# PSUM buffers for the turned x in an RWKV-6 and MLP-mixer kernel: from the pair shared with token mixing to the state products' or the grams'

## Chip, cores, metric

One core of one Trainium2 chip. The metric is the device time of one execution in microseconds, the median of several.

## The reference

```python
B, H, S, D = 4, 8, 768, 48                       # r, k, v, w: (B, H, S, D); DM = H * D = 384
for t in range(S):                               # RWKV-6, per batch and head
    cur = u * k[t] (outer) v[t]
    y[t] = r[t] @ (state + cur)
    state = w[t][:, None] * state + k[t] (outer) v[t]
x = y transposed to (B, S, H * D)
h = relu(x.T @ w_tok1) @ w_tok2                  # token mixing, d_tok = 256
u = x + h.T
out = u + relu(u @ w_ch1) @ w_ch2                # channel mixing, d_ch = 1536
```

All in fp32.

## The kernel before

It first runs the attention of batch 0 (three units of 256 tokens; twelve units in all), then for each batch the mixer, with the next batch's attention woven among it. Three pools of PSUM take all eight banks of 2 KiB (abridged; comments are mine):

```python
ps_g = tile_pool(name="ps_g", bufs=2, PSUM)   # grams: 2 buffers of [128, 2, 512] fp32, two banks each
ps_a = tile_pool(name="ps_a", bufs=1, PSUM)   # state products kv and y: 1 buffer of two banks
ps_m = tile_pool(name="ps_m", bufs=2, PSUM)   # all the rest, tag "m": 2 buffers of one bank
```

The stage of the change, for each batch `bt` (abridged; comments are mine, L428 is line 428 of the kernel):

```python
def back(c):                                  # token mixing's second product, row c (128 tokens), C = 6 rows
    ps = ps_m.tile([128, DM], f32, name="h_ps", tag="m")
    for i in range(DTOK // 128):
        pe.matmul(ps, wtok2[:, i, ts(c, 128)], h1[:, i, :], start=(i == 0), stop=(i == DTOK // 128 - 1))  # L428
    x = xs[bt]
    dve.tensor_add(x[:, c, :], x[:, c, :], ps)                                                            # L430

def turn(c):                                  # turn row c of x, for the channel products
    ps = ps_m.tile([128, DM // 128, 128], f32, name="xT_ps", tag="m")
    for m in range(DM // 128):
        pe.transpose(ps[:, m, :], xs[bt][:, c, ts(m, 128)], ident)                                        # L435
    act.copy(xT[:, :, ts(c, 128)], ps)                                                                    # L436

def up(s, jt):                                # channel mixing's first product
    ps = ps_m.tile([128, SEG], f32, name="z_ps", tag="m")                                                 # L443, L445
    ...
turned = [(1.3, lambda: back(0))]
for c in range(1, C):
    turned += [(1.3, lambda c=c: back(c)), (0.6, lambda c=c: turn(c - 1))]
turned.append((0.6, lambda: turn(C - 1)))
```

So the order is product 0, product 1, transposes 0, product 2, transposes 1, ... product 5, transposes 4, transposes 5. Then come channel products (`z_ps`) and "quarter products" (`q_ps`, `quarters`, channel mixing's second product with seven products instead of eight). The attention parts that are woven among these are small matmuls (48*64, 48*32 and 64*64 in the profile's rows, where the mixer's are 128*128): `gram`, products of k with r (L233, L250, L256), `kv_ps`, k with v for the state (L333), and `y_ps`, the attention's result (L370, L383). The turned k (`kT_ps`, L323) is a 128*128 transpose. Each engine's order is fixed when the kernel is compiled, and pieces of later work are then put where a gap is expected, as the traces show.

## Time and profile before

| | before |
|---|---|
| time, median of six runs in all | 626.71 us (625.52 to 629.18) |
| span of the profiled run | 624.1 us |
| PE idle after the first 90 us | 4.1 + 5.0 us |
| PE, batches 1 and 2, in the stage | 14.16 of 14.24, 15.86 of 16.15 us busy |

A row of the timeline gives start, length, engine, line, operation, operands, count and, in brackets, the idle time of the engine before it with what ended it. PE matmuls are pipelined: the length of a row runs to the modelled end of the last one. In the trace, one fp32 matmul of the source is two records. The page and views are in the prediction below.

### The profile page before, as it was taken

How to read it: one execution, taken by the hardware profiler on the slowest of the kernel's cores; microseconds unless marked ns; L12 is line 12 of the kernel's file. 1: busy time of each engine (PE TensorE's matmuls, PEld its weight loads, DVE VectorE, ACT ScalarE, POOL GpSimd, SP SyncE). 2: the span in 40 equal slices, each digit the busy share in tenths (PEclk: the TensorE clock that was granted, in tenths of full speed). 3: DMA queues.
4: the chain of work that ended last, by engine and by line, in shares of the span. 5: the costliest groups of instructions: out<-in, count | busy, mean ns of one | idle time of the engine just before them, and what ended most of it. 6: DMA issues, size and time to landing. Idle time of an engine off the chain costs nothing.

```text
span 624.1 us, 19852 instructions
## 1 busy us (share of the span) xinstructions
PE 591.5 (95%) x8980; PEld 500.7 (80%) x8980; DVE 341.5 (55%) x743; ACT 201.6 (32%) x500; POOL 7.2 (1%) x32
## 2 busy tenths in 40 slices
PE   2888788999999999999999999999999999999997
PEld 2867556876888896789889896789899885898987
DVE  5889799996766783436364362526243331040403
ACT  6064554520355433432323312332212411202020
POOL 4000000000000000000000000000000000000000
PEclk9996679999999999999999999999999999999999
DMA  8236564610232222111111100000000000000000
GB/s 344 105 80 213 162 197 141 221 43 27 65 94 79 54 67 66 30 50 27 53 45 60 27 28 27 1 2 3 26 2 27 2 27 1 0 1 26 16 12 26
DMA packets 19380, 38.63 MB, mean 62 GB/s; under 512 B 2112, under 2 KB 12864, under 8 KB 19296
## 3 DMA queue, kind: packets, MB, share of 16 engines
q1 hardware_dynamic: 19152, 37.36, 19.0%
q8 instruction: 70, 1.15, 0.8%
q14 instruction: 14, 0.11, 0.1%
q10 hardware_dynamic: 144, 0.00, 0.0%
HBM read 32.64 MB, written 4.72 MB: 60 GB/s over the span
## 4 chain that ended last, share of the span: by engine, by line
PE 88%; DVE 6%; ACT 3%; issue 1%; DMA 1%; SPq 0%; DVEq 0%; ACTq 0%
PE z_ps L443 30%; PE q_ps L477 25%; PE gram L256 8%; PE h_ps L428 5%; PE h_ps L421 5%; PE h_ps L453 3%; PE y_ps L383 2%; PE y_ps L370 2%; PE kv_ps L333 2%; PE gram L233 2%; PE kT_ps L323 1%; PE xT_ps L435 1%; PE gram L250 1%; DVE state L350 1%; DMA w<-in_rkw_dram 1%
## 5 line engine op out<-in xcount | busy, mean ns | idle before, releaser
L443 PE MATMUL z_ps<-xT,wch 128*128 128x256 f32 x864 | 195.3, 382 | 0.0
L443 PEld LDWEIGHTS z_ps<-xT,wch 128*128 128x128 f32 x864 | 161.4, 190 | 22.4 <-ACT z L445 0.7
L445 ACT ACTIVATE z<-z_ps 128x256 f32<-128x256 f32 x144 | 55.0, 382 | 159.4 <-PE z_ps L443 145.7
L477 PE MATMUL q_ps<-wch,z 128*128 128x192 f32 x528 | 93.6, 329 | 0.0
L477 PEld LDWEIGHTS q_ps<-wch,z 128*128 128x128 f32 x528 | 86.3, 190 | 1.3
L477 PE MATMUL q_ps<-scratch,z 128*128 128x192 f32 x396 | 71.1, 330 | 0.0
L256 PEld LDWEIGHTS gram<-r,k 48*64 48x64 f32 x3072 | 59.4, 153 | 13.0 <-issue 7.2
L256 PE MATMUL gram<-r,k 48*64 48x32 f32 x3072 | 64.6, 235 | 4.1 <-issue 1.8
L477 PEld LDWEIGHTS q_ps<-scratch,z 128*128 128x128 f32 x396 | 64.3, 190 | 0.9 <-ACT kT L324 0.2
L288 DVE TENSOR_TENSOR k<-k,decay 112x512 f32<-112x512 f32 x36 | 24.9, 691 | 46.1 <-PE gram L256 34.6
L469 DVE TENSOR_TENSOR z<-z 128x768 f32<-128x768 f32 x11 | 10.5, 958 | 63.5 <-ACT z L445 63.4
L288 DVE TENSOR_TENSOR k<-k,w 112x512 f32<-112x512 f32 x36 | 24.8, 690 | 35.6 <-PE gram L256 30.0
L428 PE MATMUL h_ps<-h,wtok 128*128 128x384 f32 x96 | 37.0, 510 | 3.8 <-DVE x L430 2.0
L350 DVE SCALAR_TENSOR_TENSOR state<-state,w_chunk,kv_ps 128x48 f32<-128x48 f32 x160 | 30.7, 258 | 17.3 <-PE kv_ps L333 17.3
L421 PE MATMUL h_ps<-x,wtok 128*128 128x384 f32 x96 | 37.5, 541 | 1.7 <-ACT x L389 1.6
L430 DVE TENSOR_TENSOR x<-x,h_ps 128x384 f32<-128x384 f32 x24 | 13.3, 555 | 36.6 <-PE h_ps L428 36.3
L233 PE MATMUL gram<-rp,kp 48*64 48x64 f32 x768 | 22.5, 248 | 10.9 <-ACT kp L221 8.2
L272 DVE COPY_PREDICATED at<-mask,gram 128x512 f32<-128x512 uint8 x36 | 32.3, 898 | 0.0
L233 PEld LDWEIGHTS gram<-rp,kp 48*64 48x64 f32 x768 | 18.4, 154 | 15.4 <-ACT kp L221 10.7
L421 PEld LDWEIGHTS h_ps<-x,wtok 128*128 128x128 f32 x96 | 19.2, 208 | 13.5 <-ACT x L389 2.0
L280 ACT COPY at<-gram 16x256 f32<-16x256 f32 x48 | 17.4, 363 | 36.3 <-PE gram L256 35.1
L428 PEld LDWEIGHTS h_ps<-h,wtok 128*128 128x128 f32 x96 | 16.4, 189 | 15.5 <-DVE x L430 3.3
(80 smaller groups left out, 563.0 us busy)
## 6 DMA issues: line engine op xcount, KB each, us to landing
scratch<-in_w_ch_dram SPq DMA_DIRECT2D x10, 512.0 KB, 4.4
vt<-in_v_dram SPq DMA_DIRECT2D x12, 384.0 KB, 3.7
out_dram<-o SPq DMA_DIRECT2D x24, 192.0 KB, 1.9
x<-in_w_ch_dram SPq DMA_DIRECT2D x8, 512.0 KB, 4.4
w<-in_rkw_dram SPq DMA_DIRECT2D x18, 192.0 KB, 3.3
k<-in_rkw_dram SPq DMA_DIRECT2D x18, 192.0 KB, 3.1
r<-in_rkw_dram SPq DMA_DIRECT2D x18, 192.0 KB, 3.5
scratch<-in_w_tok_dram SPq DMA_DIRECT2D x4, 512.0 KB, 9.2
```

Source lines behind the costliest of these rows:

```text
L233: pe.matmul(g[cols, q, ts(a, T)], L["kp"][rows, tokens], L["rp"][rows, tokens], start=True, stop=True)
L256: fours(lambda q, j, rows, cols: pe.matmul(g[cols, q, ts(ca, 32)], k_[rows, ds(ca * 128 + j * T, T)], right[rows, ts(2 * ca + j, 32 // b), ...
L272: dve.copy_predicated(out=dst, data=g.rearrange("p q (m b) -> p q m b", b=b), mask=masks[l].rearrange("p x t -> p (x t)").rearrange("p (m ...
L280: act.copy(at[p:p + b, :, :, n * 2 * b + b:(n + 1) * 2 * b], g[p:p + b, :, :, ts(n, b)])
L288: dve.tensor_mul(left, left, wv[:, :, 1].unsqueeze(2).to_broadcast([ROWS, n, b]))
L350: dve.scalar_tensor_tensor(new[:, a], state[bt, g][:, a], L["w"][:, c, a, j:j + 1], got[:, a], op0=ALU.mult, op1=ALU.add)
L421: pe.matmul(sums[i], wtok1[:, c, ts(i, 128)], xs[bt][:, c, :], start=(c == 0), stop=(c == C - 1))
L428: pe.matmul(ps, wtok2[:, i, ts(c, 128)], h1[:, i, :], start=(i == 0), stop=(i == DTOK // 128 - 1))
L443: pe.matmul(ps, wch1[:, m, ts(jt, 128)], xT[:, m, ts(s, SEG)], start=(m == 0), stop=(m == DM // 128 - 1))
L445: act.activation(zs[s][:, jt, :], ps, AF.Relu)
L453: pe.matmul(ps, zs[0][:, jt, ts(n, 128)], wch2[:, jt, :], start=(jt == 0), stop=(jt == NJ - 1))
L477: pe.matmul(ps, a[:, j, :], b[:, j, :], start=(j == 0), stop=(j == HJ - 1))
```

## The change

Intent: the product gets both small buffers for itself, so that its addition no longer holds up the next product; the transposes borrow a buffer that is free at the time. In batches 0 and 3 no attention runs beside this stage and the state buffer is free; in batches 1 and 2 state products of the next batch run there, so a gram buffer is taken.

```diff
         def turn(c):
-            ps = ps_m.tile([128, DM // 128, 128], f32, name="xT_ps", tag="m")
+
+            if bt in (0, B - 1):
+                ps = ps_a.tile([128, 2, 512], f32, name="xT_ps", tag="a")
+            else:
+                ps = ps_g.tile([128, 2, 512], f32, name="xT_ps", tag="gram")
+            ps = ps[:, 0, :DM].rearrange("p (m t) -> p m t", t=128)
             for m in range(DM // 128):
```

## The prediction

> **What bounds the kernel now.** I read first the page's busy shares and its picture by slices, and the two agree: TensorE is the bound nearly everywhere after the first 90 us.
>
> ```profile
> PE 591.5 (95%) x8980; PEld 500.7 (80%) x8980; DVE 341.5 (55%) x743; ACT 201.6 (32%) x500; POOL 7.2 (1%) x32
> ...
> PE   2888788999999999999999999999999999999997
> ...
> DVE  5889799996766783436364362526243331040403
> ...
> PEclk9996679999999999999999999999999999999999
> ```
>
> PE is idle 624.1 - 591.5 = 32.6 us in all. Cutting the span into three stretches shows where:
>
> ```profile
> 0.00:90.00 90.00, 66.61 (x1874) 54.92 (x1874) 75.26 (x175) 43.58 (x105) 6.66 (x27) 0.85 0.57 185
> 90.00:520.00 430.00, 425.86 (x6598) 357.61 (x6597) 241.70 (x524) 139.93 (x351) 0.56 (x5) 1.00 0.16 48
> 520.00:624.10 104.10, 99.06 (x511) 88.15 (x509) 24.54 (x45) 18.11 (x46) 0.00 (x0) 1.00 0.03 12
> ```
>
> The columns are the stretch, its length, then busy time of PE, PEld, DVE, ACT, POOL, the granted clock, the DMA share and GB/s. 23.4 us of the idle time lie in the first 90 us, before the changed code is first reached (its first transpose runs at 92.2 us); the change cannot touch them. Only 4.1 us lie between 90 and 520, and 5.0 us after 520 (some of that is the end of the program). So the purse is small from the start. The table of waits, restricted to PE, says which waits the changed code owns:
>
> ```profile
> PE h_ps L428 <- DVE x L430: 2.0, 6, 0.4
> ...
> PE h_ps L428 <- ACT xT L436: 1.7, 3, 0.6
> ...
> PE xT_ps L435 <- ACT xT L436: 0.6, 1, 0.6
> ...
> PE xT_ps L435 <- DVE x L430: 0.3, 1, 0.3
> ```
>
> L428 is token mixing's second product (24 of them, six for each of four batches), L430 the VectorE addition that empties it, L435 the transposes of a row of x, L436 the ScalarE copy that empties them. Products and transposes now take turns in two PSUM buffers of one bank each, which the hidden product, the channel products and, in batches 1 to 3, the turned k share too. These rows hold 4.6 us of plain idleness, but the modelled end of a pipelined matmul hides part of a wait, so I measured the steps themselves in the timeline. In the last batch, where nothing else runs beside it:
>
> ```profile
> 523.72 1.56 PE L428 MATMUL h_ps<-h,wtok 128*128 128x384 f32 x4 [0.32 <-DVE x L430]
> 524.79 0.14 PEld L435 LDWEIGHTS xT_ps<-ident,x 128*128 128x128 f32 x1
> 525.11 0.49 PE L435 MATMUL xT_ps<-ident,x 128*128 128x128 f32 x3
> 525.11 0.25 PEld L435 LDWEIGHTS xT_ps<-ident,x 128*128 128x128 f32 x2 [0.18 <-issue]
> 525.31 0.55 DVE L430 TENSOR_TENSOR x<-x,h_ps 128x384 f32<-128x384 f32 x1 [1.65 <-PE h_ps L428]
> 525.64 0.48 ACT L436 COPY xT<-xT_ps 128x384 f32<-128x384 f32 x1 [1.72 <-PE xT_ps L435]
> 525.92 0.94 PEld L428 LDWEIGHTS h_ps<-h,wtok 128*128 128x128 f32 x4 [0.56 <-DVE x L430]
> 525.92 1.56 PE L428 MATMUL h_ps<-h,wtok 128*128 128x384 f32 x4 [0.32 <-DVE x L430]
> ```
>
> The reader is to see a loop that is not bound by PE: the product begins at 523.72, its addition begins when the product is out (525.31) and ends at 525.86, and only then does the next product begin, at 525.92. The period is 2.20 us, and the two transfers of work between PE and VectorE are its whole length (1.57 for the product to come out, as the chain of work merges it, + 0.56 + the handshakes). The next product reads nothing that this addition writes; it waits only for the buffer.
>
> **What the Trainium skill says.** "Perfetto Trace Analysis", section Optimization Strategy: a gap that repeats on the engine that should be saturated can mean that there is no PSUM for the next tile. The trace agrees: four gaps of 0.32 to 0.39 us with one releaser in the last batch. The same page, section Matmuls: independent matmul groups should rotate through different banks so that emptying one overlaps the next group. That is what the change does. "PSUM — Partial Sum Buffer", Specifications: 8 banks of 2 KiB for each partition. All eight are taken here (two gram buffers of two banks, one state buffer of two, two of one bank), so the change can only borrow, not add. "TensorE: Matmul & The Clock Gate", Part 4: a 128x128 transpose takes some 275 ns in a kernel, for bf16. Here, in fp32, the median is 273 ns, as a latency; three in a row take 0.49 us.
>
> **The change part by part.** No instruction is added or removed: 72 transposes, 24 copies and 24 additions stay. The operand shapes and strides of transposes and copies stay as well. What moves is which buffer each waits for.
>
> *The product* rotates through two buffers of its own; product c+1 waits for addition c-1, which ran during product c. The wait is gone.
>
> *The transposes* of row c-1 need addition c-1 (data) and the buffer. I read the length of an unhindered step from the trace: from a product's start to the first transpose 525.11 - 523.72 = 1.39 us, and from a transpose's start to the next work on PE, where PE did not have to wait, 0.42 us:
>
> ```profile
> 396.27 0.49 PE L435 MATMUL xT_ps<-ident,x 128*128 128x128 f32 x3
> ...
> 396.69 0.45 PE L370 MATMUL y_ps<-state,r 48*64 48x48 f32 x16
> ```
>
> So a step falls from 2.20 to 1.39 + 0.42 = 1.81 us. The addition's 0.55 us and the copy's 0.48 us both fit inside it, even with the single state buffer.
>
> *Last batch.* First transpose of row 0 to that of row 4: 522.91 to 531.79, 8.88 us for four steps; now 4 x 1.81 = 7.24, a gain of 1.64. Row 5's transposes follow row 4's with no product between, 0.82 us later. They must wait for addition 5 in any case, and with one state buffer also for copy 4 (about 0.5 + 0.48 + 0.05 = 1.05 us). But a channel product, which needs only rows 0 and 1 and now finds a free buffer, can be put in front of them; then this joint costs PE 0.42, a gain of 0.40. Together 2.0 us. If nothing is put in front, the joint costs about 0.24 more than before, and the gain is 1.4.
>
> *First batch.* The waits are longer, for here a product shares its buffer with a transpose and waits for the copy:
>
> ```profile
> 95.01 0.49 PE L435 MATMUL xT_ps<-ident,x 128*128 128x128 f32 x3
> ...
> 95.54 0.48 ACT L436 COPY xT<-xT_ps 128x384 f32<-128x384 f32 x1 [1.98 <-PE xT_ps L435]
> ...
> 96.07 1.56 PE L428 MATMUL h_ps<-h,wtok 128*128 128x384 f32 x4 [0.57 <-ACT xT L436]
> ```
>
> Rows 0 to 4 take 92.56 to 102.12, 9.56 us; four unhindered steps are 7.24, a gain of 2.32. The joint to row 5 takes 1.06 instead of 0.42, a gain of 0.64. That makes 2.96. But VectorE is 12.35 us busy in these 14.07 us, with the conversion of the weights, and an addition can stand behind two conversion steps of 0.68 us. The slack of a transpose is about one product, 1.3 us, so now and then one will be late. I choose to take off 0.5: 2.4 us.
>
> *Batches 1 and 2.* The waits were already filled with the next batch's attention matmuls: between 246.35 and 260.59 PE is busy 14.16 of 14.24 us, between 386.10 and 402.25 15.86 of 16.15. That filled work is not saved, it moves. What can be gained is 0.1 + 0.3 us of idleness and some changes from one matmul shape to another (about 0.1 us each). What can be lost: the transposes now take one of two gram buffers, which a gram holds until its masked copy is through (1.30 us, behind other VectorE work). I set the net of both at 0.3 us gained.
>
> The sum is 2.0 + 2.4 + 0.3 = 4.7 us. All three sit on the chain that ends last (the chain of work goes through L428 and L430 there), and after each stage PE is the bound and stays so, which is why I carry the gains to the end undiminished. 627.08 - 4.7 = 622.4 us.
>
> **Rivals.** *A new wait in the gram buffers.* In batches 1 and 2 a gram or a transpose stands in PE's fixed order behind a buffer that VectorE frees late. For it: the trace shows grams already waiting for masked copies (L272, 1.7 us in three waits). Against: six transposes for each of two batches, and other work around. Two waits of 1 us in each batch would cost 4 us and leave about 623 + 3.5 = 626.5. *VectorE gives the first batch's gain back.* It is 100% busy from 103.5 to 135 us, so if the channel products needed weights sooner than they are converted, PE would stop later. Against it: the last pair of conversions that the fifth column block of the first channel product needs ends at 102.3, and that block begins near 114, a margin of nearly 12 us; 3 us fewer still leave 9. If it did, the time would be about 625. *The order of work changes elsewhere.* The matmuls of several stages are interleaved in a compiled order that depends on when buffers come free; with other buffers it may come out better or worse by a microsecond or two, also far from the change. That would give 620 to 625. *Fillers are worth more than I think:* in batches 1 and 2 each chunk of state products, broken into pieces by the waits, costs changes of shape; whole chunks could give another microsecond, 621.
>
> **Range and chances.** The three times before spread from 625.52 to 629.18, so the median is good to about a microsecond. The gain should be between 1.5 us (rival one, or the low joints) and 7.3 us (all of 2.0 + 3.0 with a good new order). That is 619.8 to 625.6. Two per cent would be 12.5 us, more than all PE idleness after 90 us (9.1 us), so faster by 2% would need a different order in the first 90 us, and slower by 2% a wait that recurs dozens of times; the code runs 24 times.
>
> **What would show it.** Right: the rows L428 waiting for L430 or L436 vanish; the period of the last batch's steps is 1.8 us; the stage from the first product to the first channel product in the last batch shrinks from 12.87 to about 10.9 us, the first batch's from 14.07 to about 11.5; a channel product stands between the transposes of rows 4 and 5. Wrong: L435 waiting for L272, L280 or L239, or grams waiting for L436, by more than 1 us in all; a period still over 2 us; batches 1 and 2 longer than before; or PE idle between 135 and 240 us where it was busy. If the stages shrink as said and the time does not, something later takes the gain back.

## The result, and the profile after

618.28 us, median of six runs (614.5 to 618.99), against 626.71 of the kernel before: a ratio of 0.9852 (95% interval 0.9821 to 0.9882). The ratio is the mean time of the one kernel's runs over that of the other's of the same rounds, so not quite the ratio of the medians. Within 2%, as forecast, but 8.4 us instead of 4.7, and below the range. In two later sets of rounds the ratios were 0.9832 and 0.9857.

(In the changed kernel, lines after L433 are five further: L435 is L440, L436 L441, L443 L448, L445 L450.) The last batch's stage, from the timeline of the changed kernel:

```profile
520.67 1.46 PE L428 MATMUL h_ps<-h,wtok 128*128 128x384 f32 x4
520.87 0.48 ACT L441 COPY xT<-xT_ps 128x384 f32<-128x384 f32 x1 [1.14 <-PE xT_ps L440]
521.64 0.14 PEld L440 LDWEIGHTS xT_ps<-ident,x 128*128 128x128 f32 x1
521.97 0.49 PE L440 MATMUL xT_ps<-ident,x 128*128 128x128 f32 x3
521.97 0.25 PEld L440 LDWEIGHTS xT_ps<-ident,x 128*128 128x128 f32 x2 [0.18 <-issue]
522.17 0.56 DVE L430 TENSOR_TENSOR x<-x,h_ps 128x384 f32<-128x384 f32 x1 [1.06 <-PE h_ps L428]
522.18 0.95 PEld L428 LDWEIGHTS h_ps<-h,wtok 128*128 128x128 f32 x4
522.29 1.46 PE L428 MATMUL h_ps<-h,wtok 128*128 128x384 f32 x4
```

No bracket stands behind a product any more. The next product begins at 522.29, while the addition of the last one still runs (522.17 to 522.73). The period is 522.29 - 520.67 = 1.62 us, not 1.81. The weights of the product are loaded 0.11 us before it begins (522.18), under the transposes; before the change both began at the same moment, when the buffer came free.

The busy times of PE (the first figure after the comma), in the stages of batches 0, 2 and 3 of the changed kernel, from the first product to the first channel product:

```profile
91.86:101.59 9.73, 9.66 (x40) 5.88 (x40) 8.29 (x17) 5.86 (x13) 0.00 (x0) 1.00 0.53 157
...
383.75:398.02 14.27, 14.27 (x278) 10.01 (x277) 8.12 (x24) 4.82 (x12) 0.00 (x0) 1.00 0.01 2
515.94:525.53 9.59, 9.59 (x40) 5.89 (x39) 2.90 (x6) 2.40 (x5) 0.00 (x0) 1.00 0.01 2
```

The stage of batch 2 contains the same matmuls as before (24 and 18 of the product and the transposes, 64 of kv, 122 of gram, 48 of y), and was nearly full before (15.86 us busy of 16.15). It is now 14.27 long: 1.88 us are gone, and only 0.29 of that was idleness. That was not in the 0.3 us that I had set for it. PE's rows of this stage show where the same matmuls stood before the change:

```profile
393.74 0.49 PE L435 MATMUL xT_ps<-ident,x 128*128 128x128 f32 x3
394.16 0.78 PE L370 MATMUL y_ps<-state,r 48*64 48x48 f32 x22
394.87 1.56 PE L428 MATMUL h_ps<-h,wtok 128*128 128x384 f32 x4
```

and after it:

```profile
393.61 0.49 PE L440 MATMUL xT_ps<-ident,x 128*128 128x128 f32 x3
393.93 1.46 PE L428 MATMUL h_ps<-h,wtok 128*128 128x384 f32 x4
395.23 0.49 PE L440 MATMUL xT_ps<-ident,x 128*128 128x128 f32 x3
395.65 1.01 PE L370 MATMUL y_ps<-state,r 48*64 48x48 f32 x43
```

Before, a piece of attention work (here 22 matmuls of y) stood between a row's transposes and the next product. Now the product follows 0.32 us after the transposes begin, and y comes almost whole, after the last product.

To see which batch the time comes from, I take start-to-start distances from the trace's records. The channel products of batches 0, 1 and 3 now begin before the last transposes, so the measure runs further, from the first product of a batch to its first quarter product, which covers nearly the same work:

| from first product to first quarter product, us | batch 0 | batch 1 | batch 2 | batch 3 | sum of gains |
|---|---|---|---|---|---|
| before | 62.26 | 34.90 | 35.15 | 28.41 | |
| after | 58.57 | 33.32 | 33.27 | 25.46 | |
| gain | 3.69 | 1.58 | 1.88 | 2.95 | 10.1 |
| predicted | 2.4 | 0.3 for both | | 2.0 | 4.7 |

The whole from the first product of batch 0 to the last matmul fell from 530.9 to 521.3 us, by 9.5. The spans of the two traces differ by only 7.1, because the changed kernel reached its first product later. The compiled order of PE is the same up to there. The granted clock differed there; the row by slices of the changed kernel has one slice of 0.5 where that of before has 0.6 and 0.6 where it has 0.7:

```profile
PEclk9995669999999999999999999999999999999999
```

That is no explanation yet: over all the traces the moment lies between 88.2 and 91.9 us, in three traces of the changed kernel alone at 88.2, 88.7 and 91.9, and it does not follow the time at half clock (e2, e5, e6 and e8 below have the least of it, 14 us ahead of the first product, and arrive at 90.1 to 90.6). I leave the cause of this scatter open. It puts up to 3.7 us between the spans of two traces, so below I compare from the first product on.

### The profile page after: what moved, and what is told of

Read it like the earlier page. It is cut to its first block, busy times and chain, and to the rows that moved or that the text cites. A ratio compares the mean times of both kernels' runs of the same rounds, so it can differ in the third digit from the quotient of the medians.

```text
span 617.0 us, 19870 instructions
## 1 busy us (share of the span) xinstructions
PE 589.8 (96%) x8980; PEld 501.5 (81%) x8980; DVE 341.7 (55%) x743; ACT 201.4 (33%) x500; POOL 7.2 (1%) x32
## 4 chain that ended last, share of the span: by engine, by line
PE 86%; DVE 7%; ACT 3%; DMA 2%; issue 2%; SPq 0%; DVEq 0%; ACTq 0%
PE z_ps L448 29%; PE q_ps L482 25%; PE gram L256 8%; PE h_ps L421 6%; PE h_ps L428 5%; PE h_ps L458 3%; PE y_ps L383 2%; PE y_ps L370 2%; PE kv_ps L333 2%; PE gram L233 2%; PE kT_ps L323 1%; PE xT_ps L440 1%; PE gram L250 1%; DMA scratch<-in_w_ch_dram 1%; DMA w<-in_rkw_dram 1%
## 5 line engine op out<-in xcount | busy, mean ns | idle before, releaser
L448 PE MATMUL z_ps<-xT,wch 128*128 128x256 f32 x864 | 196.0, 383 | 0.1
L448 PEld LDWEIGHTS z_ps<-xT,wch 128*128 128x128 f32 x864 | 161.3, 190 | 22.4 <-ACT z L450 1.2
L450 ACT ACTIVATE z<-z_ps 128x256 f32<-128x256 f32 x144 | 54.9, 381 | 156.2 <-PE z_ps L448 142.4
L256 PEld LDWEIGHTS gram<-r,k 48*64 48x64 f32 x3072 | 60.1, 156 | 11.6 <-issue 6.0
L256 PE MATMUL gram<-r,k 48*64 48x32 f32 x3072 | 65.0, 237 | 3.4 <-DVE at L272 1.7
L421 PE MATMUL h_ps<-x,wtok 128*128 128x384 f32 x96 | 40.0, 570 | 1.7 <-ACT x L389 1.5
L350 DVE SCALAR_TENSOR_TENSOR state<-state,w_chunk,kv_ps 128x48 f32<-128x48 f32 x160 | 30.6, 256 | 16.5 <-PE kv_ps L333 16.5
L428 PE MATMUL h_ps<-h,wtok 128*128 128x384 f32 x96 | 35.4, 493 | 0.1
L233 PE MATMUL gram<-rp,kp 48*64 48x64 f32 x768 | 22.5, 248 | 10.6 <-ACT kp L221 7.9
L272 DVE COPY_PREDICATED at<-mask,gram 128x512 f32<-128x512 uint8 x36 | 32.3, 897 | 0.0
L421 PEld LDWEIGHTS h_ps<-x,wtok 128*128 128x128 f32 x96 | 20.3, 221 | 14.5 <-issue 3.6
L233 PEld LDWEIGHTS gram<-rp,kp 48*64 48x64 f32 x768 | 18.3, 154 | 15.1 <-ACT kp L221 10.4
L430 DVE TENSOR_TENSOR x<-x,h_ps 128x384 f32<-128x384 f32 x24 | 13.3, 554 | 28.3 <-PE h_ps L428 27.9
L289 DVE TENSOR_TENSOR r<-r,w 112x512 f32<-112x512 f32 x36 | 24.6, 686 | 4.1 <-ACT rp L217 4.1
```

The lines of the kernel that those rows point to most:

```text
L233: pe.matmul(g[cols, q, ts(a, T)], L["kp"][rows, tokens], L["rp"][rows, tokens], start=True, stop=True)
L256: fours(lambda q, j, rows, cols: pe.matmul(g[cols, q, ts(ca, 32)], k_[rows, ds(ca * 128 + j * T, T)], right[rows, ts(2 * ca + j, 32 // b), ...
L272: dve.copy_predicated(out=dst, data=g.rearrange("p q (m b) -> p q m b", b=b), mask=masks[l].rearrange("p x t -> p (x t)").rearrange("p (m ...
L289: dve.tensor_mul(right, right, wv[:, :, 0].unsqueeze(2).to_broadcast([ROWS, n, b]))
L350: dve.scalar_tensor_tensor(new[:, a], state[bt, g][:, a], L["w"][:, c, a, j:j + 1], got[:, a], op0=ALU.mult, op1=ALU.add)
L421: pe.matmul(sums[i], wtok1[:, c, ts(i, 128)], xs[bt][:, c, :], start=(c == 0), stop=(c == C - 1))
```

## The experiments

Runs of one group ran on one chip and in the same rounds. "From the first product" is the time from batch 0's first product to the last matmul. A "visit" is one passage of PE from 128*128 matmuls into attention matmuls and back, counted in the trace's matmul records from the first product on. (The expectations below count visits in the compiled order of the whole program, which are 9 more in each kernel that they name: 87 before the change, 79 after.)

| run | median us | ratio to before (95%) | from the first product, us | visits |
|---|---|---|---|---|
| before (first trace) | 626.71 | | 530.9 | 78 |
| after (first trace) | 618.28 | 0.9852 (0.9821 to 0.9882) | 521.3 | 70 |
| a_again, the change | 616.78 | 0.9832 (0.9813 to 0.9851) | 521.0 | 70 |
| e1_last | 623.85 | 0.9948 (0.9928 to 0.9968) | 527.9 | 78 |
| e2_first | 623.18 | 0.9933 (0.9917 to 0.9949) | 527.4 | 78 |
| e3_middle | 623.92 | 0.9955 (0.9939 to 0.9971) | 527.5 | 70 |
| e4_product | 628.72 | 1.0039 (1.0012 to 1.0067) | 532.3 | 72 |
| e5_chunks | 621.21 | 0.9926 (0.9902 to 0.9950) | 525.2 | 82 |
| e6_gram | 619.43 | 0.9887 (0.9857 to 0.9917) | 524.7 | 71 |
| e7_state | 620.26 | 0.9904 (0.9879 to 0.9929) | 525.3 | 74 |
| a_third, the change | 616.90 | 0.9857 (0.9835 to 0.9879) | 521.5 | 70 |
| e8_keys | 611.60 | 0.9760 (0.9734 to 0.9785) | 515.7 | 56 |

The ten runs of this section gave correct results. The groups: a_again to e3; e4 to e7; the last two. Before had a median of 626.72, 626.25 and 626.13 in them. The second group holds no run of the changed kernel, so e4 to e7 are set against it by their traces and by their ratios to before.

**The change again, and its three parts.** Theory: an unhindered step is 1.62 us, and a visit of attention matmuls costs PE time even where PE never waits. Rivals: the gain comes from a new order of work elsewhere; VectorE gives the first batch's gain back; the gram buffers bring a new wait.

> The changed kernel once more, on the chip that runs the three parts below, as their measure. Both theories: about 8 us under the kernel before (it was 8.4 us by medians). In the trace I look at each batch's stage from the first product to the first quarter product: 58.6, 33.3, 33.3 and 25.5 us in the first trace of it, against 62.3, 34.9, 35.2 and 28.4 before. They should repeat within 0.2 us. The arrival at the first product in the first batch (91.9 us after, 89.5 before) should scatter by a few us with the windows of half clock before it: if it is always later in the changed kernel than before, the change costs something early that I do not see.

Stages 58.75, 33.32, 33.27 and 25.46 us: they repeat. The first product came at 88.7 us, earlier than in the trace before the change (89.5), so the change has no steady cost in the early part.

e1, e2, e3 each keep one branch. This is e1 against the kernel before; e2 has `(0,)` in the first condition, and e3 has `()` in the first and `(1, 2)` in the second:

```diff
-            ps = ps_m.tile([128, DM // 128, 128], f32, name="xT_ps", tag="m")
+
+            if bt in (B - 1,):
+                ps = ps_a.tile([128, 2, 512], f32, name="xT_ps", tag="a")
+                ps = ps[:, 0, :DM].rearrange("p (m t) -> p m t", t=128)
+            elif bt in ():
+                ps = ps_g.tile([128, 2, 512], f32, name="xT_ps", tag="gram")
+                ps = ps[:, 0, :DM].rearrange("p (m t) -> p m t", t=128)
+            else:
+                ps = ps_m.tile([128, DM // 128, 128], f32, name="xT_ps", tag="m")
```

> The change in the last batch alone. My theory after the result (an unhindered step is 1.62 us, not the 1.81 that I composed): the stage of the last batch shrinks by 2.9 us, the other three stay as before; the time falls by 2.9. The prediction as put on record: 2.0. Rival, the stages were helped by the new order of work far away rather than by their own buffers: less than 1.

Batch 3's stage is 25.46 us (from 28.41, a gain of 2.95), the others stay within 0.05 of before; 0.9948 is 3.3 us.

> The change in the first batch alone. My theory: that stage shrinks by 3.7 us, the time by 3.7 less what the following stretch gives back (0.2 to 0.5 in the first pair of traces). The prediction: 2.4, because additions would stand behind conversions. Rival (VectorE gives it back): the stage shrinks, the time does not.

Batch 0's stage is 58.63 us (from 62.26, 3.63 gained), the others as before; 0.9933 is 4.2 us. VectorE gives nothing back.

> The change in batches 1 and 2 alone, with the gram buffers. My theory (each visit of attention matmuls among the 128-wide ones costs PE 0.33 us, and the compiled order has 79 such visits instead of 87): 8 x 0.33 + 0.3 us of idleness + a weight load or two = 3.2 to 3.5 us shorter. The prediction: 0.3. Rival (gram buffers make a new wait): longer than before.

33.31 and 33.27 us (from 34.90 and 35.15: 1.59 + 1.88 = 3.47 gained); 0.9955 is 2.8 us, and 3.4 counted from the first product.

The stages' gains add up: 2.95 + 3.63 + 3.47 = 10.05, against 9.92 in a_again and 10.10 in the first trace. The ratios add up too (0.52 + 0.67 + 0.45 = 1.64%, against 1.68%). So each part acts where it stands; no distant order explains the result. The waits of PE in a_again, from 85 to 520 us, hold one row (total us, times, longest us), and none in the changed lines or for their new buffers:

```profile
PE kT_ps L323 <- DVE k L288: 0.8, 2, 0.5
```

**Which side needs the two buffers.** e4 is the mirror: `turn` keeps `ps_m`, `back` takes the borrowed buffers.

```diff
         def back(c):
-            ps = ps_m.tile([128, DM], f32, name="h_ps", tag="m")
+            if bt in (0, B - 1):
+                ps = ps_a.tile([128, 2, 512], f32, name="h_ps", tag="a")
+            else:
+                ps = ps_g.tile([128, 2, 512], f32, name="h_ps", tag="gram")
+            ps = ps[:, 0, :DM]
```

> The mirror: the product takes the state buffer (first and last batch) or the gram buffers (batches 1 and 2), the transposes keep the two small buffers for themselves. If what counts is only that product and transposes no longer share, the steps are 1.62 us and the time is as for the change (about 8 us under before). My theory: the product needs two buffers, because product c+1 is ready before addition c has ended; with the single state buffer the period in the first and last batch stays at 2.2 us or more and only the middle gains: 1 to 4 us under before.

Not merely no gain, but 2.5 us over before. Batches 0 and 3 keep the old period, with the same wait, for a product with one buffer must let its addition end first (here L432 is the product and L434 the addition):

```profile
526.82 1.56 PE L432 MATMUL h_ps<-h,wtok 128*128 128x384 f32 x4 [0.32 <-DVE x L434]
...
529.02 1.24 PE L432 MATMUL h_ps<-h,wtok 128*128 128x384 f32 x3 [0.32 <-DVE x L434]
```

And product 1 now waits for addition 0 as well (0.65 us in batch 3), which it did not before. I had expected the middle to gain; its period fell to 1.62 us in many steps, but the sum of batches 1 and 2 and what follows them was no shorter than before (367.9 us from batch 0's first quarter product to batch 3's first product, against 368.3 before and 364.9 in a_again). Most of the middle's loss stands in the trace. Three products there wait for VectorE, 0.62 us for L350 (the state), 0.80 and 0.52 for L239 and L272 (the masked copies that empty grams), 1.94 us in all where the changed kernel has no such wait, and there are two visits more, some 0.7 us. That makes 2.6 of the 3.0 us; the rest is not traced. The separation alone is not the point: in batches 0 and 3 the long chain (product, addition) must be the one that rotates, and in the middle the product must not stand behind grams.

**What a visit costs.** From start-to-start distances in the changed kernel's trace (medians): a channel product's matmul follows its like by 216 ns, but an attention matmul follows it by 309 ns (93 more); from the last attention matmul to the next 128*128 one it is 149 ns (attention matmuls follow each other by some 15 ns on average: 134 more); and the second 128*128 matmul after a visit comes 321 ns after the first, not 216 (105 more). Together 0.33 us. e5 makes more visits without making any wait (abridged, comments are mine; `ca` counts the pairs of c and a):

```diff
-        def before():                 # y = r @ state, one piece of weight 1.1
+        def before(ca4):              # the same matmuls, in four pieces of weight 0.275 where bt > 0
             ...
-            for c in range(UC):
-                for a in range(A):
+            for ca in range(2 * ca4, 2 * ca4 + 2):
+                c, a = divmod(ca, A)
```

> The changed kernel with the first half of the state products of units 3 to 11 cut in four pieces that are woven apart. Nothing waits more; the compiled order has 91 visits of attention matmuls among the others instead of 79. My theory (0.33 us for each visit, read from start-to-start times: 93 ns going in, some 134 coming out, some 100 for the first weight load after): 12 x 0.33 = 4.0 us longer than the changed kernel, with no new wait on PE. Rival (filling PE's gaps with attention work is free, as I assumed when I set the middle batches to 0.3): as the changed kernel within 1 us.

From the first product it took 525.2 us, against 521.0 to 521.5 of the changed kernel: 4.0 more, or 0.33 for each of the 12 added visits, with the same single row of waits on PE between 100 and 520 us. The loss stands where the visits are: against a_again, 1.38 us for four more between batch 1's first quarter product and batch 2's first product, and 1.70 for five more between those of batches 2 and 3. Filling gaps is not free.

**Other choices of buffer.**

> All four batches take a gram buffer, of which there are two. If the single state buffer costs the joint between the transposes of rows 4 and 5 (a wait for copy 4), this is faster than the change by up to 0.5 us in the first and last batch; if channel products stand in that joint, as the traces show, it is the same within 0.3 us.

The joint between transposes 4 and 5 did shrink (0.90 us instead of 1.19, with fewer channel products in it), but batch 0's stage is 61.79 us instead of 58.7, 3.1 longer. It is not a wait: in the changed kernel two grams of the next batch (128 matmul records, 64 of L256 and 64 of L233) stand before batch 0's first product, where PE is idle anyway; with the transposes in the gram buffers they stand after it. At some 1.06 us each, as a gram of 64 takes in the chain of work, and with the one visit more, that accounts for 2.5 of the 3.4 us lost from the first product on; the rest I did not trace.

> All four batches take the state buffer. In batches 1 and 2 it also holds the state products of the next batch, for several us at a time. My theory: transposes and state products now wait for each other there; the compiled order has 83 visits; the time is 2 to 4 us over the changed kernel. Rival, the compiled order avoids the clash: within 1 us of the changed kernel.

Some 4.1 us longer than the changed kernel from the first product on (525.3); the stages of batches 1 and 2 are 35.51 and 35.38. Four visits more are 1.3 us; the transposes (here L443) wait for the state buffer until ScalarE has copied y out of it (L389):

```profile
PE xT_ps L443 <- ACT x L389: 1.6, 2, 0.9
```

One row's transposes come 11.1 us after the last ones in batch 1, 13.4 us in batch 2; other work fills most of it. Some 1.2 us of the loss are not resolved. So both branches of the change are needed, each for its own reason.

**A version that beats both.** If visits cost that much, take away more of them. The two groups of four k transposes of a unit wait for small buffers too, and the compiled order put grams between them. In e8 both groups of a unit take the two halves of one state buffer; the next user of that buffer, kv, needs the turned k in any case.

```diff
-            if bt == 0:
-                both = ps_g.tile([128, 2, 512], f32, name="gram").rearrange("p c (a t) -> p c a t", a=A)
+            pool_, tag_ = (ps_g, "gram") if bt == 0 else (ps_a, "a")
+            both = pool_.tile([128, 2, 512], f32, name="gram" if bt == 0 else "kT_ps", tag=tag_)
+            both = both.rearrange("p c (a t) -> p c a t", a=A)
             for c in range(UC):
-                ps = both[:, c] if bt == 0 else ps_m.tile([128, A, 128], f32, name="kT_ps", tag="m")
+                ps = both[:, c]
```

> The changed kernel as the measure for the next run, on the same chip and in the same rounds. About 8 to 10 us under the kernel before; the four stages 58.6 to 58.8, 33.3, 33.3 and 25.5 us again.

> The changed kernel, and in units 3 to 11 the turned k takes both halves of one state buffer too, in place of two of the small buffers. The compiled order has 65 visits of attention matmuls instead of 79, for the two groups of k transposes need no fillers any more. My theory (0.33 us for each visit): 14 x 0.33 = 4.6 us under the changed kernel. Rival (filling is free): the same within 1 us. Second rival (the state buffer, now shared by three kinds of product, makes state products wait): over the changed kernel.

611.6 us against 616.9 in the same rounds; from the first product 515.7 against 521.5, 5.8 less for 14 visits less. That is 0.41 a visit, or 4.6 us at 0.33 and 1.2 us for which I have no single cause (0.2 us of it is less waiting on PE). Between batch 0's first quarter product and batch 1's first product, where e8 has seven visits less and the same matmuls, it is 1.9 to 2.5 us shorter than the three traces of the changed kernel, 0.28 to 0.35 a visit; the unexplained part lies in the later batches. The view of the last two of three stretches shows that PE was busy before and is busy after: the gain is in the last stretch's length, not in PE's share (PE's busy time and matmuls are again the first pair after the comma).

```profile
90.00:520.00 430.00, 428.94 (x6648) 360.94 (x6647) 246.10 (x534) 143.62 (x359) 0.56 (x5) 1.00 0.16 49
520.00:609.80 89.80, 86.44 (x463) 80.72 (x461) 21.23 (x39) 15.03 (x40) 0.00 (x0) 1.00 0.04 14
```

For comparison, the same view of the changed kernel:

```profile
90.00:520.00 430.00, 428.70 (x6616) 359.77 (x6616) 244.78 (x531) 141.48 (x354) 0.56 (x5) 1.00 0.17 49
520.00:617.00 97.00, 93.60 (x497) 85.81 (x495) 23.45 (x43) 17.14 (x44) 0.00 (x0) 1.00 0.04 13
```

Within the same busy 430 us, PE got through 32 matmuls more (6648 against 6616), and 34 fewer are left for the end. (The first product of this e8 trace came at 90.4 us, of this trace of the changed kernel at 91.9; 1.5 us of the difference in span are that.)

## Why the prediction was wrong

Right in mechanism, in sign and in most of its marks: the waits of L428 for L430 and L436 vanished, a channel product stands between the transposes of rows 4 and 5, nothing waits for the gram buffers, and PE keeps the gain to the end. The sizes of the terms were wrong. The stages gained 10.1 us where I had 4.7; of the 5.4 us between, 3.2 are in batches 1 and 2, 1.3 in batch 0 and 0.95 in batch 3:

- **The unhindered step, predicted 1.81 us, is 1.62.** This is the step that failed first: "a step falls from 2.20 to 1.39 + 0.42 = 1.81 us". I put it together from two places in the old trace and took both for unhindered. The 1.39 us came from a product that had waited, so that its first weights were loaded in the open: its first matmul is followed by the next after 0.426 us, not 0.323. The 0.42 us came from transposes followed by an attention matmul, the passage into a different shape of PE work, which costs 93 ns. The sum of the plain distances is 4 x 0.323 + 3 x 0.109 = 1.62, which the trace before would have given. Four steps gain 8.88 - 6.48 = 2.40 us in the last batch, where I had 1.64, and 9.56 - 6.48 = 3.08 in the first, where I had 2.32.
- **The joint**: I had 0.40 (last) and 0.64 (first). In the last batch it is now 1.19 us, with four channel matmuls of 0.216 in it, so 0.33 of its own, from 0.81: a gain of 0.48. Right to a tenth.
- **VectorE in the first batch**: I took off 0.5 us for additions that come late (2.96 - 0.5 is 2.46, which I wrote as 2.4). Nothing was late enough to be seen: PE waits for no addition there, and e2 gains 3.63 us.
- **Batches 1 and 2, predicted 0.3 us for both, gained 3.47.** This is the largest miss. The step was "That filled work is not saved, it moves", with "some changes from one matmul shape to another (about 0.1 us each)", which I neither counted nor measured. The work does move, but it moved in whole pieces instead of being broken into pieces: 8 visits fewer at 0.33 us are 2.6 us, the idleness of 0.1 and 0.3 us is 0.4, together 3.0; the other 0.5 would be weight loads that waits had exposed, but that I did not separate. e5 measured the cost by itself. (The masked copy's 1.30 us, which I set against this gain, is the longest of L272; the median is 0.71.)
- **The bound on the gain.** I held that 2% was out of reach because PE is idle for only 9.1 us after the first 90. Idleness does not bound the gain, for PE's busy time shrinks too: e8 is 14.5 us under before (ratio 0.9760) with PE's order in the first 90 us unchanged.

Three rivals fell: no wait for gram buffers, no gain given back by VectorE (e2), and no new order far from the change (the parts add up). "Fillers are worth more than I think" was the rival that held, though I gave it one microsecond where it was worth about three. The medians of the first set show 8.4 us and not the stages' 10. In its traces 0.5 us is lost again between batches 0 and 1 (a_again does not repeat that) and 2.4 us by the later first product; the later sets, with an earlier first product in their traces, have 9.9 and 9.2 us between the medians.

## What to carry to other kernels

When two kinds of work share a pair of PSUM buffers, give the pair to the one whose emptying is on its own critical chain and let the other borrow any buffer that is idle in that phase; ask for each phase which one that is. A profile that shows the bound engine busy does not show that it is well used: a wait filled with other work costs the passage into that work and back, so count those passages, and measure them start to start. And build the length of an unhindered step from distances inside runs of like instructions, not from pieces that follow a wait or lead into other work.

## What the Trainium skill lacked or had wrong

- "TensorEngine Tiling (Array Packing)", Key Properties: it says that a change of tiling mode drains TensorE, which I should have looked up before I predicted. The traces here show time lost at each change of matmul shape, which fits; that a drain takes it, and not the first weight load, no run here separates. The page lacks the size: from fp32 matmuls of 128*128 into the small ones (48*64, 48*32 or 64*64) and back costs 93 + 134 + 105 = 0.33 us, and 12 added passages cost 4.0 us in e5. The changed kernel makes 70 of them after its first product, which is about 23 us of its 617 (an estimate, 70 x 0.33); taking 14 away gained 5.8 us.
- "TensorE: Matmul & The Clock Gate", Part 4: it gives some 275 ns for a transpose in a kernel, as the record of one has here (273 ns, fp32); but transposes in a row begin 109 ns apart here, which Part 4 does not give, and which is the figure that counts on a busy PE.
